# Unit 8's q and k moved to the transposing transfer, with unit 9's behind unit 7's x

## The chip, the cores and the metric

The kernel runs on one core of a Trainium2 chip. A core has five engines with their own instruction streams: TensorE (PE, matrix products into PSUM), VectorE (DVE), ScalarE (ACT), GpSimd (POOL) and SyncE (SP). They wait for one another through semaphores. Data moves between device memory and the on-chip SBUF over 16 DMA engines; in this kernel POOL issues the loads (one DMA queue, q0 in the profile) and SP issues the stores and the transposing transfers (another queue, q1). The metric is the device time of one execution in microseconds; lower is better.

## The reference

Attention inside chunks of 64 tokens, and then a feed-forward layer on its result:

```python
q_c = q.reshape(B, H, nc, chunk, D)          # B=8, H=8, S=576, D=64, chunk=64
k_c = k.reshape(B, H, nc, chunk, D)
v_c = v.reshape(B, H, nc, chunk, D)
scores = scale * np.matmul(q_c, k_c.transpose(0, 1, 2, 4, 3))
scores = scores - np.max(scores, axis=-1, keepdims=True)
attn = np.exp(scores)
attn = attn / (np.sum(attn, axis=-1, keepdims=True) + 1e-09)
out = np.matmul(attn, v_c)
...
x = out.transpose(0, 2, 1, 3).reshape(B * S, H * D)      # 4608 x 512
h = x @ w_in                                             # 4608 x 2048
g = h * (1.0 / (1.0 + np.exp(-beta * h)))
return g @ w_out                                         # 4608 x 512
```

## The kernel before

The 4,608 tokens are cut into 18 units of 256 tokens (units 0 to 17); two units make a block of 512 tokens (blocks 0 to 8). Unit u belongs to block u // 2, so units 6 and 7 make block 3, units 8 and 9 block 4.

A unit's attention goes through these steps:

- `load_qk` and `load_v`: POOL issues transfers that read q, k and v of the unit from device memory and turn them into fp16 tiles (`qu`, `ku`, `vbig`). The q and k tiles have four buffers each, so the loads of unit u + 4 wait until the tiles of unit u have been transposed; `emit_T(u)` ends with `loads_to(u + 4)`.
- `emit_T`: q and k are transposed so that the head dimension lies on partitions (`qT`, `kT`, three buffers each). There are two ways. Up to unit XU - 1 DVE does it with two stream transposes of 32x32 squares (L164), and q and k are loaded in the layout for that, two neighbouring tokens in one row (L112). From unit XU on SP issues two transposing transfers (`dma_start_transpose`, L159), and the loads use another layout, with 128 tokens on partitions (L106).
- `emit_sc`: the scores. With the squares of the first way PE needs 64 matmuls, each over 32 rows, two accumulating into one result (L232). With the second way it needs 32 matmuls over 64 rows (L219). ACT then takes the exponential (L241 or L225) into `et`.
- `emit_pv`: weights times v, with a column of the sum (L256 for units 8 and up; `xe` and `x` in PSUM). The scores and this product share one PSUM tile, tag "s".
- `emit_norm`: DVE divides by the sums and leaves `x16`.
- `emit_xt_dma`: SP issues two transposing transfers per unit (L348) that bring x into the layout `xt` that the feed-forward layer reads.

A block's feed-forward layer has 16 tiles: `emit_m(j, m)` is four matmuls of 128x512 over `xt` and w_in (L372, `hps`), the gate on ACT (L384) and DVE (L360), into `gt`. The second layer of the previous block runs at the same time: `emit_prod(j - 1, p, t)`, seven products p with two halves t each (a Strassen-like scheme that saves one product of eight), eight matmuls of 128x256 per half (L585, `ya` and `yb`; `acc` in block 1). A half takes 0.87 us on PE, a tile the same.

The order is written out by hand. For each block j from 1 on, `items` is a list of (due, rank, item), due being a fraction of the block; it is sorted by due and rank, and items with the same pair keep the order in which they were added. All engines receive their instructions in that order, each its own part. Tile m of a middle block is due at m0 + (1 - m0) * m / 16; half t of the i-th product at 0.98 * (2 * i + t) / 14. For blocks 3 to 5 the table `ATT` places the attention of units 8 to 17; unit u's entry there also places `("T", u + 3)` for u from 8 on, so units 11 and up get their transposes from there. Units 6 to 10 are placed one by one in block 2's list.

SP works off its queue in order: for block 2 that is, before the change, unit 6's x (78.38 us), unit 9's kT and qT (81.25, 82.58), unit 7's x (87.76), a store, unit 10's kT and qT (92.84, 94.54), a store, unit 11's (99.04, 102.38).

Of the kernel before, what the change touches and what calls it, by code (L numbers as in the profile page):

```python
# [15 lines left out]
def kernel(  # L16
# [59 lines left out]

    blocks = [(u, 2) for u in range(0, NU, 2)]
    NB = len(blocks)
    XU = 9
    WV = 8  # L80
    QB = 6
    unit_block = {}
# [15 lines left out]
    def load_qk(u):  # L98
        for src, dst, nm in ((q, q_t, "qu"), (k, k_t, "ku")):
            t = qk_p.tile([128, H, 2, D], FP16, tag=nm, name=nm)  # L100
            if u >= XU:
                dst[u] = t
# [49 lines left out]
    def emit_T(u, which=("kT", "qT")):  # L152
        for nm in which:
# [3 lines left out]
            dst[u] = t  # L157
            if u >= XU:
                nc.sync.dma_start_transpose(  # L159
# [50 lines left out]
    def emit_sc(u, split=False):  # L210
        qt, kt = qT.pop(u), kT.pop(u)
        sc = ps_s[0].tile([128, 2, H, CH], FP32, tag="s", name="sc")
        if u >= XU:
            qx, kx = (t.rearrange("p h s e -> p (h s e)").rearrange("p (j c t) -> p j c t", j=H, c=2)
# [29 lines left out]
    def emit_pv(u, halves=(0, 1)):  # L244
        et = et_t[u]
        if u >= WV:
# [3 lines left out]
            for n in (7, 0, 1, 2, 3, 4, 5, 6):  # L250
                for r in range(2):
# [3 lines left out]
                    for c in range(2):  # L255
                        nc.tensor.matmul(  # L256
                            out=o[64 * c:64 * c + 64],
                            lhsT=(et[64 * r:64 * r + 64, g % 2, 4 * s + 2 * c + g // 2, :] if u >= XU
                                  else et[64 * r:64 * r + 64, s, 4 * c + g, :]),
# [354 lines left out]
    with tc.manual_schedule():  # L614
# [123 lines left out]
        for j in range(1, NB):  # L738
            if j == 3:
                ps_open.pop().__exit__(None, None, None)  # L740
                ps_open.pop().__exit__(None, None, None)
                ps_open += [tc.tile_pool(name=n, bufs=1, space=bass.MemoryType.PSUM) for n in ("ps_y", "ps_t")]
                ps_y.append(ps_open[-2].__enter__())
                ps_s[0] = ps_open[-1].__enter__()
            items = []
            if j == 1:
                items += [(0.04 * m, 0, ("h", m)) for m in range(8)]
                items += [(0.32 + 0.0820 * (m - 8), 0, ("m", m)) for m in range(8, KFF)]
                items += [(0.30, 3, ("T", 4)), (0.49, 2, ("sc", 4)), (0.70, 2, ("pv", 4)), (0.71, 3, ("norm", 4, 0)),
                          (0.80, 3, ("norm", 4, 1)), (0.56, 3, ("Th", 5, "kT")), (0.61, 3, ("Th", 5, "qT"))]  # L750
                items += [(c, 3, ("wt", i)) for i, c in ((1, 0.47),)]
            else:
                m0 = {2: 0.36, 4: 0.09}.get(j, 0.02)
                if j < QB:
                    items += [(m0 + (1 - m0) * m / KFF, 0, ("m", m)) for m in range(KFF)]
                else:
                    lane = LANE[2 if j == QB else j == NB - 1]
                    cost = [1 if it[0] == "q" and it[2] == 3 else 2 for it in lane]
                    for n, it in enumerate(lane):
                        c, e, f = (0.98 * sum(cost[:n + d]) / sum(cost) for d in (0, 1, 2))  # L760
                        items.append((c, 0, it))
                        if it[0] == "m":
                            items.append((c + 0.04, 3, ("mg", it[1])))
                        elif it[0] == "last":
                            pass
                        elif it[2] == 2:
                            if it[1] == 3:
                                f = e
                            items += [(e - 0.002, 2, ("qs", it[1], 2)), (f - 0.001, 2, ("qs", it[1], 1)),
                                      (f + 0.03, 3, ("qt", it[1], 0))]  # L770
                        elif it[2] == 3:
                            items += [(c + 0.001, 2, ("qs", it[1], 0)), (c + 0.04, 3, ("qt", it[1], 1))]
                    if j == QB:
                        items.append((0.01, 6, ("open",)))
                        items += [(0.011+0.001*n, 6, ("tx", QB, n)) for n in range(4)]
                    if j + 1 < NB:
                        items += [(0.70 + 0.06 * n, 5, ("tx", j + 1, n)) for n in range(4)]
                for i, p in enumerate((1, 2, 6, 5, 7, 3, 4)):
                    for t in range(2):
                        w = 1.06 if j == NB - 1 else 0.98  # L780
                        items.append(((0.002 if j >= QB else 0) + w * (2 * i + t) / 14, 1, ("prod", p, t)))
                if j == NB - 1:
                    for i, c in ((2, 0.72), (0, 0.80), (1, 0.86)):
                        items.append((c, 4, ("pre", i)))
                for i in range(4):
                    s0 = (0.01, 0.08, 0.28, 0.36)[i] if j == 2 else 0.005 + 0.07 * i
                    if j >= QB:
                        s0 = (0.08, 0.15, 0.33, 0.48)[i] if j == QB else (0.003, 0.10, 0.33, 0.48)[i]
                    items.append((s0, 4, ("sum", i)))
                if j == 2:  # L790
                    items += [(c, 3, ("wt", i)) for i, c in ((2, 0.36), (3, 0.55))]
                    items += [(0.07, 2, ("sc", 5)), (0.08, 2, ("xp", 4, 0)), (0.12, 2, ("xp", 4, 1)),
                              (0.17, 2, ("pv", 5)), (0.18, 3, ("norm", 5, 0)), (0.19, 3, ("norm", 5, 1)),
                              (0.27, 3, ("T", 6)), (0.53, 3, ("T", 7)), (0.60, 3, ("T", 8)), (0.61, 3, ("T", 9)), (0.80, 3, ("T", 10)),
                              (0.30, 2, ("xp", 5, 0)), (0.32, 2, ("xp", 5, 1))]
                for jw, i, c, d in ((3, 2, 0.10, 0.22), (4, 1, 0.21, 0.22), (4, 3, 0.10, 0.22)):
                    if jw == j:
                        items += [(c + d * n, 5, ("ws", i, n)) for n in range(4)]
                for u, a0, w in ATT.get(j, ()):
                    items += att_items(u, a0, w)  # L800
            items.sort(key=lambda it: it[:2])
            for _, _, it in items:
                if it[0] == "m":
                    emit_m(j, it[1])
                elif it[0] == "h":
                    emit_m(j, it[1], 256, 256)
                elif it[0] == "prod":
                    emit_prod(j - 1, it[1], it[2])
                elif it[0] == "pre":
                    emit_sum(j, it[1], 0, 8 if it[1] == 2 else 4)  # L810
                elif it[0] == "sum":
                    emit_sum(j - 1, it[1])
                elif it[0] == "sc":
                    emit_sc(it[1])
                elif it[0] == "pv":
                    emit_pv(it[1], (0, 1) if len(it) == 2 else (it[2],))
                elif it[0] == "norm":
                    emit_norm(it[1], it[2])
                    if it[1] not in (4, 5):
                        emit_xt_dma(it[1], it[2])  # L820
                elif it[0] == "xp":
                    emit_xt_pe(it[1], it[2])
                elif it[0] == "wt":
                    emit_wt(it[1], (1,))
                elif it[0] == "last":
                    emit_prod(j, it[1], it[2])
                elif it[0] == "q":
                    emit_q(j, it[1], it[2])
                elif it[0] == "qs":
                    emit_q_silu(j, it[1], it[2])  # L830
                elif it[0] == "qt":
                    emit_q_scale(j, it[1], it[2])
                elif it[0] == "mg":
                    emit_mg(j, it[1])
                elif it[0] == "ws":
                    emit_ws(it[1], it[2])
                elif it[0] == "open":
                    ps_open.pop().__exit__(None, None, None)
                    ps_open.append(tc.tile_pool(name="ps_r", bufs=2, space=bass.MemoryType.PSUM))
                    ps_p[0] = ps_open[-1].__enter__()  # L840
                    while att_open:
                        att_open.pop().__exit__(None, None, None)
                    qs_p.append(ctx.enter_context(tc.tile_pool(name="qh", bufs=3)))
                    qs_p.append(ctx.enter_context(tc.tile_pool(name="qs", bufs=1)))
                    osl_p.append(ctx.enter_context(tc.tile_pool(name="osl", bufs=6)))
                elif it[0] == "tx":
                    emit_tx(it[1], it[2])
                elif it[0] == "Th":
                    emit_T(it[1], (it[2],))
                elif it[1] < NU:  # L850
                    emit_T(it[1])
# [39 lines left out]
```

## Time and profile before

| | us |
|---|---|
| median of three runs | 275.39 (275.33 to 276.52) |
| the profiled execution's own time | 276.16 |
| its span, first to last instruction | 274.4 |
| PE busy | 266.0 |
| DVE busy | 209.7 |
| ACT busy | 167.5 |
| POOL busy | 95.4 |
| granted TensorE clock | 1.000 |

The profile is one execution. Times within it are microseconds from the start of its span; the span is 1.8 us shorter than the execution's own time, and that execution is 0.8 us above the median of the runs. PE's matmuls are pipelined, so in a timeline the start of the next group, and not the end of one, tells what a group costs. "q0 software_dynamic" in the DMA view is the queue of POOL's loads, "q1 hardware_dynamic" that of SP's transfers; the columns are packets, MB, and the time that the packets took as a share of 16 engines' time (packets overlap, so shares over 100% occur).

Where the attention of the units lies on PE: scores of unit 8 at 96.26, 9 at 105.35, 10 at 115.86, 11 at 125.51, 12 at 134.28, 13 at 144.79, 14 at 155.30, 15 at 163.21, 16 at 171.99 and 17 at 179.90. First tiles: block 3 at 96.97, block 4 at 126.77, block 5 at 154.35.

### The profile page before, as it was taken

Reading aid. Unit: us, or ns where it says so; the run is one execution under the profiler, and the core shown is the slowest. Engines: PE = TensorE matmul, PEld = TensorE weight load, DVE = VectorE, ACT = ScalarE, POOL = GpSimd, SP = SyncE. Lnnn points to the kernel's source line nnn. Section 1 sums busy time; section 2 is a strip of 40 time slices with the busy share of each in tenths; the row PEclk is TensorE's granted clock in tenths of the full one; section 3 lists DMA queues with packets and bytes.
Section 4 is the critical chain, followed back from the end, with each engine's and each line's share of the span. In section 5 each row is a group of like instructions: output and inputs, shape, how many; then the busy total and the mean of one; then the engine's idle time right before and its main releaser. Section 6 shows DMA issues by size and latency. Waiting matters only on the chain.

```text
span 274.4 us, 7822 instructions
## 1 busy us (share of the span) xinstructions
PE 266.0 (97%) x3237; PEld 184.9 (67%) x3237; DVE 209.7 (76%) x394; ACT 167.5 (61%) x300; POOL 95.4 (35%) x122
## 2 busy tenths in 40 slices
PE   7789999999999999999999999999999999999995
PEld 3565445857656666666666666668887887788874
DVE  3558755899998688677977887659888778877951
ACT  3278515886555566556655656567778496759621
POOL 8954387579639955323436210000000000000000
PEclk9999999999999999999999999999999999999999
DMA  9999999999999999999999999966112102110223
GB/s 137 164 194 202 192 174 178 245 169 169 169 164 155 159 173 153 193 145 141 155 154 193 134 143 201 153 155 118 38 41 76 41 0 79 38 41 1 78 79 115
DMA packets 141763, 36.43 MB, mean 133 GB/s; under 512 B 125856, under 2 KB 141216, under 8 KB 141728
## 3 DMA queue, kind: packets, MB, share of 16 engines
q0 software_dynamic: 99136, 18.10, 83.0%
q1 hardware_dynamic: 42592, 17.84, 36.4%
q8 instruction: 25, 0.41, 0.6%
q14 instruction: 10, 0.08, 0.1%
HBM read 36.71 MB, written 9.44 MB: 168 GB/s over the span
## 4 chain that ended last, share of the span: by engine, by line
PE 67%; DMA 14%; DVE 10%; POOL 5%; issue 2%; ACT 2%; DVEq 0%; POOLq 0%
PE hps L372 23%; PE ya L585 14%; PE yb L585 14%; PE qx L484 5%; DMA wout<-in_moe_w_out_dram 5%; PE qz L484 4%; PE acc L585 4%; DMA qu<-in_q_dram 3%; DMA win<-in_moe_w_in_dram 3%; DMA ku<-in_k_dram 3%; DVE sm L436 3%; DVE gt L360 2%; POOL vbig L120 2%; PE sc L219 1%; POOL qu L112 1%
## 5 line engine op out<-in xcount | busy, mean ns | idle before, releaser
L372 PE MATMUL hps<-xt,win 128*128 128x512 f16 (+1 forms) x488 | 106.1, 355 | 0.9 <-DMA win<-in_moe_w_in_dram 0.7
L384 ACT ACTIVATE sg<-hps,bt 128x512 f32<-128x512 f32 (+1 forms) x111 | 69.5, 635 | 34.3 <-PE hps L372 31.9
L360 DVE SCALAR_TENSOR_TENSOR gt<-sg,hps 128x512 f16<-128x512 f32 (+1 forms) x111 | 67.7, 617 | 27.1 <-ACT sg L384 26.2
L372 PEld LDWEIGHTS <-win 128*128 128x128 f16 x488 | 46.2, 98 | 32.3 <-DMA win<-in_moe_w_in_dram 1.2
L585 PEld LDWEIGHTS <-sm 128*128 128x128 f16 x512 | 49.5, 98 | 12.2 <-issue 0.3
L585 PEld LDWEIGHTS <-gt 128*128 128x128 f16 x384 | 36.8, 98 | 10.6 <-DVE gt L527 0.6
L120 POOL DMA_DIRECT2D vbig<-in_v_dram x40 | 34.1, 870 | 21.8 <-DMA ku<-in_k_dram 6.3
L106 POOL DMA_DIRECT2D qu<-in_q_dram x20 | 17.1, 873 | 20.6 <-DMA qT<-qu 6.0
L513 ACT ACTIVATE hq<-hq,bs 128x256 f32<-128x256 f32 (+1 forms) x36 | 19.9, 610 | 5.5 <-DVE hq L506 5.5
L527 DVE TENSOR_SCALAR gt<-hq,rb 128x512 f16<-128x512 f32 x36 | 16.2, 481 | 6.0 <-ACT hq L513 5.3
L106 POOL DMA_DIRECT2D ku<-in_k_dram x20 | 17.1, 883 | 10.2 <-DMA qu<-in_q_dram 5.1
L436 DVE TENSOR_TENSOR sm<-gt 128x2048 f16<-128x2048 f16 (+1 forms) x17 | 19.6, 1155 | 0.3
L585 PE MATMUL yb<-wt,sm 128*128 128x256 f16 x152 | 19.7, 273 | 0.1
L585 PE MATMUL ya<-wt,sm 128*128 128x256 f16 x152 | 19.7, 273 | 0.0
L484 PEld LDWEIGHTS <-ws 128*128 128x128 f16 x144 | 14.1, 98 | 1.6
L241 ACT ACTIVATE et<-sc 128x1024 f16<-128x1024 f32 (+1 forms) x10 | 8.3, 852 | 10.5 <-PE sc L232 10.4
L397 PE MATMUL ops<-wout,gt 128*128 128x512 f16 x64 | 14.7, 380 | 0.0
L585 PE MATMUL yb<-wout,gt 128*128 128x256 f16 x104 | 13.9, 273 | 0.2
L585 PE MATMUL ya<-wout,gt 128*128 128x256 f16 x104 | 13.6, 273 | 0.0
L506 DVE TENSOR_TENSOR hq<-qz,hq 128x512 f32<-128x512 f32 x18 | 12.3, 683 | 1.1 <-ACT hq L503 0.8
L503 ACT COPY hq<-qx 128x512 f32<-128x512 f32 x18 | 10.5, 581 | 2.9 <-PE qx L484 2.7
L278 DVE TENSOR_TENSOR x<-x,rx 128x512 f16<-128x512 f32 (+1 forms) x20 | 11.9, 620 | 0.3
(100 smaller groups left out, 354.3 us busy)
## 6 DMA issues: line engine op xcount, KB each, us to landing
out_dram<-osb SPq DMA_DIRECT2D x32, 256.0 KB, 2.9
vbig<-in_v_dram POOLq DMA_DIRECT2D x32, 128.0 KB, 7.6
qu<-in_q_dram POOLq DMA_DIRECT2D x18, 128.0 KB, 11.5
ku<-in_k_dram POOLq DMA_DIRECT2D x18, 128.0 KB, 8.3
win<-in_moe_w_in_dram POOLq DMA_DIRECT2D x8, 256.0 KB, 9.5
wout<-in_moe_w_out_dram POOLq DMA_DIRECT2D x4, 512.0 KB, 12.2
qu<-in_q_dram POOLq DMA_DIRECT2D x5, 256.0 KB, 6.5
ku<-in_k_dram POOLq DMA_DIRECT2D x5, 256.0 KB, 6.8
```

The source lines that it names most:

```text
L106: nc.gpsimd.dma_start(out=tv[off:off + n, sp], in_=src[b, :, s:s + n, :].rearrange("h p d -> p h d"),)
L120: nc.gpsimd.dma_start(out=vbig[off:off + n, i % NV, :, 0:D], in_=v[b, :, s:s + n, :].rearrange("h p d -> p h d"),)
L360: nc.vector.scalar_tensor_tensor(out=gt_t[j][:, m, c0:c0 + n], in0=sg[:, 0:n], scalar=1.0, in1=hps[:, 0:n], op0=ALU.add, op1=ALU.mult,)
L372: nc.tensor.matmul(out=hps[:, 0:n], lhsT=w_in16[m // 2][:, kk, (m % 2) * 128:(m % 2) * 128 + 128], rhs=xr[:, c0 // CH:(c0 + n) // CH, 2 * ...
L384: nc.scalar.activation(out=sg[:, 0:n], in_=hps[:, 0:n], func=ACTF.Tanh, scale=bt[:, m:m + 1])
L397: nc.tensor.matmul(out=ops, lhsT=gt_t[j][:, kk, t * 128:(t + 1) * 128], rhs=w_out16[kk // 4][:, kk % 4, :], start=(kk == 0), stop=(kk == K ...
L436: nc.vector.tensor_tensor(out=sm[i][:, lo:hi, :], in0=a, in1=b, op=op)
L484: nc.tensor.matmul(out=dst[:, s, :], lhsT=lhsT, rhs=rhs, start=(p in (1, 2, 5) and s == 0 and kk == 0), stop=(s == 1 and kk == 1), skip_gr ...
L506: nc.vector.tensor_tensor(out=o, in0=x if p == 7 else z, in1=o, op=ALU.add)
L513: nc.scalar.activation(out=o, in_=src, func=ACTF.Silu, scale=bs[:, m:m + 1])
L527: nc.vector.tensor_scalar(out=gt_t[j][:, m, :], in0=hq[:, b].rearrange("p c q -> p (c q)"), scalar1=rb[:, m:m + 1], scalar2=None, op0=ALU. ...
L585: nc.tensor.matmul(out=dst, lhsT=lhsT, rhs=rhs, start=(p in (1, 2, 5) and kk == 0 and (t == 0 or last)), stop=(kk == 7 and (t == 1 or last ...
```

## The change

Three edits:

1. XU goes from 9 to 8: unit 8's q and k are loaded in the other layout and transposed by two transposing transfers on SP; its scores are 32 matmuls.
2. In block 2's list, `("T", 8)` is due at 0.53, right behind `("T", 7)`, and `("T", 9)` at 0.79, behind unit 7's last `norm` and its x.
3. Block 3's tiles begin at m0 = 0.09, where they began at 0.02.

```diff
-    XU = 9
+    XU = 8
...
-                m0 = {2: 0.36, 4: 0.09}.get(j, 0.02)
+                m0 = {2: 0.36, 3: 0.09, 4: 0.09}.get(j, 0.02)
...
-                              (0.27, 3, ("T", 6)), (0.53, 3, ("T", 7)), (0.60, 3, ("T", 8)), (0.61, 3, ("T", 9)), (0.80, 3, ("T", 10)),
+                              (0.27, 3, ("T", 6)), (0.53, 3, ("T", 7)), (0.53, 3, ("T", 8)), (0.79, 3, ("T", 9)), (0.80, 3, ("T", 10)),
```

In the instruction streams this gives: on PE 32 score matmuls in place of 64, and at the start of block 3 the order product half, scores of unit 8, product half, first tile, weighted sum of unit 8 (before: product half, scores, first tile, product half, second tile, weighted sum); on DVE two stream transposes fewer; on POOL four load instructions for unit 8's q and k in place of two; on SP the order unit 6's x, unit 8's kT and qT, unit 7's x, a store, unit 9's, unit 10's, a store, unit 11's, and from there as before.

## The prediction

> **What bounds the kernel now.** I read the page first: the busy times, then the row of DMA slices.
>
> ```profile
> PE 266.0 (97%) x3237; PEld 184.9 (67%) x3237; DVE 209.7 (76%) x394; ACT 167.5 (61%) x300; POOL 95.4 (35%) x122
> ...
> DMA  9999999999999999999999999966112102110223
> ```
>
> PE is idle for 8.4 us of the span of 274.4, so the end is set by the sum of PE's work plus whatever makes PE wait. The DMA engines are busy in the first 26 of 40 slices (to 178 us), which is the whole stretch that the change touches. So there are two resources without room. Next, the view by stretches of time, to see where PE idles:
>
> ```profile
> 80.00:90.00 10.00, 9.88 (x150) 5.87 (x149) 8.96 (x16) 5.18 (x8) 7.74 (x11) 1.00 1.91 156
> 90.00:100.00 10.00, 10.00 (x154) 6.24 (x151) 7.10 (x11) 6.53 (x10) 9.53 (x11) 1.00 2.16 170
> ```
>
> Second column PE: 9.88 and 10.00 of 10 us, at a granted clock of 1.00. There is no idle time left to win here, only PE work to remove. PE's timeline shows what the scores of a unit cost in each form (unit 8 by L232, unit 9 by L219):
>
> ```profile
> 95.30 1.04 PE L585 MATMUL yb<-wout,gt 128*128 128x256 f16 x8
> 96.26 0.71 PE L232 MATMUL sc<-qT,kT 32*64 32x64 f16 x64
> 96.97 1.02 PE L372 MATMUL hps<-xt,win 128*128 128x512 f16 x4
> ...
> 104.39 1.04 PE L585 MATMUL yb<-wt,sm 128*128 128x256 f16 x8
> 105.35 0.44 PE L219 MATMUL sc<-qT,kT 64*64 64x64 f16 x32
> 105.73 1.04 PE L372 MATMUL hps<-xt,win 128*128 128x512 f16 x4
> ```
>
> Starts count, as ends overlap. Then SP's timeline, the one queue that issues all transposing transfers (first column start, second how long SP was held):
>
> ```profile
> 81.25 1.23 SPq L159 DMA_TRANSPOSE kT<-ku  x1
> 82.58 1.77 SPq L159 DMA_TRANSPOSE qT<-qu  x1
> 87.76 4.28 SPq L348 DMA_TRANSPOSE xt<-x  x2
> 92.09 0.58 SPq L539 DMA_DIRECT2D out_dram<-osb  x1
> 92.84 1.60 SPq L159 DMA_TRANSPOSE kT<-ku  x1
> 94.54 3.69 SPq L159 DMA_TRANSPOSE qT<-qu  x1
> ...
> 167.75 2.70 SPq L159 DMA_TRANSPOSE kT<-ku  x1
> 170.56 2.60 SPq L159 DMA_TRANSPOSE qT<-qu  x1
> ```
>
> These are units 9, 10 and 17, with unit 7's x between. From 92.84 to about 154 SP runs with hardly a gap. Last, the DMA view for single stretches: 84 to 85 us, 106 to 110, 160 to 162 (packets, MB, share):
>
> ```profile
> q1 hardware_dynamic: 1029, 0.25, 120.5%
> ...
> q0 software_dynamic: 1716, 0.22, 82.5%
> q1 hardware_dynamic: 1646, 0.41, 78.9%
> ...
> q0 software_dynamic: 2405, 0.30, 238.0%
> ```
>
> The transposes' queue (q1) alone moves some 1,000 packets per us, the loads' queue (q0) alone 1,200; with work in both, each gets about 412 to 430. They take turns, so each slows the other.
>
> **The change part by part.** *PE.* 64 score matmuls of unit 8 (L232) become 32 (L219). From the product's start to the next group: 96.97 - 95.30 = 1.67 with L232, 105.73 - 104.39 = 1.34 with L219. Saved: 0.33 us, all on the path, since PE is full.
>
> *DVE* loses the two stream transposes of unit 8 (0.70 + 0.67 at 83.66). PE did not wait for DVE after them, so 0; the bound on the other side is a rival below.
>
> *POOL.* Unit 8's loads are four issues instead of two: units 8 and 9 took 1.81 and 3.63 us, so 1.8 us more. POOL waits 1.52 us before unit 10's loads (72.64) and 4.36 before unit 11's (82.26); that hides it. In packets, 2,048 of 256 B become 4,096 of 128 B: at 961 in 1.5 us (61 to 62.5) and 2,446 in 2 us (71 to 73) that is 3.2 against 3.35 us; from 82 to 84 the loads' queue moves nothing, which hides the 0.15. Without that cover it would delay later loads by 0.15 us.
>
> *SP.* Two transposes are added in all. Unit 8's take the place of unit 9's at 81.25, with the same neighbours, and land as those did (kT after 4.3 us; the queue was empty again by 87), against unit 8's scores at 96.26: 0. Unit 9's move behind unit 7's x, to 92.84, and units 10 and 11 and everything later on SP slide back. In unit 10's present place qT takes 10.4 us to land, at 104.9; unit 9's scores are due at 105.35 - 0.33 = 105.0. But POOL now holds unit 13's loads (94.15) until unit 9's q has been read, so fewer loads compete and I expect it near 102.5: 0, at worst 0.3.
>
> *The slide.* One unit's q and k are 2,048 packets (84 to 87 us shows 2,085 for unit 9). They are put into a stretch where both queues are full up to 169 us. Price of the slide, both ends: alone, 2,048 / 1,029 = 2.0 us; taking turns throughout, 2,048 / 412 = 5.0 us on the transposes' queue, and on the loads' 5.0 - 2,048 / 1,200 = 3.3. The rows from 105 to 170 look like the dear end, while POOL's hold makes unit 9's second half run alone; and unit 17's k, whose landing releases the issue at 167.75, now loses the stretch 160 to 162 in which it had the engines to itself. I take 4.2, between 3.3 and 5.0.
>
> *What has room for it.* Landings are issue plus the view's time to landing; dues are PE's starts less 0.33 saved and 0.3 to get going. Block 4's first tile: x of unit 9 lands at 113.1 + 8.5 = 121.6, due 126.1, room 4.5. Block 5's: 142.5 + 7.4 = 149.9, due 153.7, room 3.8. Scores of unit 15: 157.9, due 162.6, room 4.7. Unit 16: 158.62 + 10.3 = 168.9, due 171.4, room 2.5. Unit 17: 170.56 + 6.5 = 177.1, due 179.3 (its L219 group started at 179.90), room 2.2. Stalls do not add: once PE has waited, the later dues move with it. So the stall is the largest lack: 4.2 - 2.2 = 2.0 us at unit 17's scores (ends: 0 with a slide of 2.0, 2.8 with 5.0). After that PE's work is the same as before and the end moves by all of it.
>
> *Block 3's tiles.* The first tile now starts at 95.30 + 0.87 + 0.47 + 0.87 = 97.5, where unit 7's x has landed (90.8 + 5.4 = 96.2). The price is a shorter cover for unit 8's exponential: one product and one tile between scores and weighted sum. Unit 11 has that order already (125.51 to 127.73) with no gap on PE: 0, at worst 0.3.
>
> *Sum:* -0.33 + 2.0 = +1.7 us. In the profiled execution the span would go from 274.4 to 276.1; its own time is 276.16, with 1.8 around the span, so 277.9. The median of the runs shown, 275.39, lies 0.77 below that execution; put on the median, the forecast is 277.1 us.
>
> [...]
>
> **The rivals.** *The slide is hidden.* If the extra packets run mostly while the loads are held (unit 13's, for some 4 us after 100), the slide is 2.0, under the smallest room, 2.2. Then only the saved PE time shows: 275.39 - 0.33 = 275.06. For it: SP waits for other things than room at 157.28 and 167.75 and could catch up. Against: those two waits are for k to land, and the loads slide too.
>
> *The slide breaks in at several places* (slower still): if each loss feeds back, because late transposes hold POOL's next loads (the buffers have four units), the slide grows to some 6 or 7 us. It decides from 4.5 on, where blocks 4 and 5 start late as well; 6.5 - 2.2 - 0.33 = +4.0: 279.4. For it: the loads of units 13 to 16 land 11 to 19 us after issue, already. Against: unit 14's loads were issued at 105.5, 27 us ahead of their transposes.
>
> *DVE was pacing PE.* If the 1.37 us taken off DVE came back on PE, -0.33 - 1.37 = 273.7. Against: PE 9.88 and 10.00 of 10 in these stretches.
>
> That the change does not do what it says I rule out: the changed program's instruction order has 32 matmuls for unit 8 and the two more transposes.
>
> **How the numbers follow.** Forecast (277.1, own range 276.3 to 278.3) 0.50; hidden (275.06) 0.32; several places 0.14; DVE 0.04. A measurement of this kernel tells from no change about 0.5%, 1.4 us. Of the forecast's 0.50, 0.08 lies under 276.8. Slower: 0.42 + 0.14 = 0.56; same: 0.32 + 0.08 = 0.40; faster 0.04. The range reaches from just under the hidden case to near the several-places case: 274.9 to 279.0.
>
> **What would show it.** Right: unit 8's scores in about 0.47 us of PE; unit 9's transposes issued near 92.8 and its scores unhindered; unit 17's issued near 171 to 173 instead of 167.75, and a PE gap of 1 to 3 us ahead of its scores, the only large one. Wrong: no gap there (hidden); gaps at the first tiles of blocks 4 and 5 (several places); or a gap at unit 9's scores, which would mean that its place behind unit 7's x is too late.

## The result, and the profile after

| | before | after |
|---|---|---|
| median of six runs, us | 275.64 (275.33 to 276.52) | 278.04 (277.12 to 281.62) |
| profiled execution's own time, us | 276.16 | 278.86 |
| its span, us | 274.4 | 277.1 |

After over before is 1.0081, with a 95% interval of 1.0054 to 1.0109: slower by 0.5 to 1.1%. Ratios, here and below, leave out executions in a slower state, of which 281.62 is one. The medians differ by 2.4 us, where 1.7 were forecast; the median of after lies in the forecast's range and 0.9 above the forecast. Where the time went is another matter.

The page of after, the same two rows as before:

```profile
PE 266.9 (96%) x3205; PEld 185.0 (67%) x3205; DVE 208.9 (75%) x392; ACT 167.3 (60%) x300; POOL 97.2 (35%) x124
...
DMA  9999999999999999999999999965112102110223
```

32 matmuls fewer, and the row of nines is the same. The view by stretches of after (columns: stretch, its length, then busy time and number of instructions of PE, PEld, DVE, ACT and POOL, the granted clock, DMA share, GB/s):

```profile
80.00:90.00 10.00, 9.88 (x150) 5.82 (x148) 7.98 (x15) 5.65 (x8) 6.73 (x9) 1.00 1.92 150
90.00:100.00 10.00, 10.00 (x127) 6.53 (x126) 7.65 (x15) 6.08 (x11) 5.26 (x6) 1.00 2.22 167
120.00:130.00 10.00, 8.54 (x120) 5.74 (x119) 6.96 (x13) 5.29 (x9) 2.92 (x4) 1.00 1.73 142
150.00:160.00 10.00, 8.37 (x104) 5.16 (x105) 7.16 (x13) 5.27 (x11) 3.90 (x5) 1.00 1.60 164
```

Before's lines of the last two stretches:

```profile
120.00:130.00 10.00, 10.00 (x157) 6.64 (x146) 8.49 (x19) 5.51 (x11) 2.93 (x4) 1.00 1.77 138
150.00:160.00 10.00, 10.00 (x127) 6.58 (x126) 8.59 (x18) 6.44 (x13) 3.40 (x4) 1.00 1.76 142
```

PE lost 1.46 and 1.63 us in two stretches where it was full before; from 80 to 120, from 130 to 150 and from 160 to 190 it is as full as it was. PE's timeline of after names the spots: unit 8's scores, then the first tiles of blocks 4 and 5 (in square brackets the idle time just before, and what the profile puts it down to):

```profile
94.50 1.04 PE L585 MATMUL yb<-wout,gt 128*128 128x256 f16 x8
95.47 0.45 PE L219 MATMUL sc<-qT,kT 64*64 64x64 f16 x32
95.85 1.05 PE L585 MATMUL yb<-wout,gt 128*128 128x256 f16 x8
...
127.28 1.02 PE L372 MATMUL hps<-xt,win 128*128 128x512 f16 x4 [1.46 <-DMA xt<-x]
...
156.65 1.02 PE L372 MATMUL hps<-xt,win 128*128 128x512 f16 x4 [1.63 <-issue]
```

From product to next group, unit 8's scores take 95.85 - 94.50 = 1.35 us, where the forecast had 1.34. The two waits are for x: of unit 9 (block 4) and of unit 11 (block 5). For the second the profile names nothing ("issue"), but the landing below does. SP's timeline of after:

```profile
80.45 2.18 SPq L159 DMA_TRANSPOSE kT<-ku  x1
82.74 2.51 SPq L159 DMA_TRANSPOSE qT<-qu  x1
86.96 4.27 SPq L348 DMA_TRANSPOSE xt<-x  x2
...
92.03 1.49 SPq L159 DMA_TRANSPOSE kT<-ku  x1
93.62 3.16 SPq L159 DMA_TRANSPOSE qT<-qu  x1
...
114.66 4.37 SPq L348 DMA_TRANSPOSE xt<-x  x2
...
146.25 2.59 SPq L348 DMA_TRANSPOSE xt<-x  x2
...
171.09 2.82 SPq L159 DMA_TRANSPOSE kT<-ku  x1
```

Units 8 and 9 are where they were expected. Of unit 11's x, the second transfer by itself, from the view of the tile `xt` (start of the issue, then time to landing); after first:

```profile
L348 SPq DMA_TRANSPOSE xt<-x x1: 1229/1229/1229, 147.6 to 147.6; - x1
...
DMA to landing us min/median/max: 8.9/8.9/8.9
```

and before:

```profile
L348 SPq DMA_TRANSPOSE xt<-x x1: 1249/1249/1249, 142.5 to 142.5; - x1
...
DMA to landing us min/median/max: 7.4/7.4/7.4
```

Unit 11's x lands at 147.6 + 8.9 = 156.5 instead of 149.9, and PE's tile starts 0.15 us later. In the same way unit 9's second transfer (117.3 + 9.9, before 113.1 + 8.5) lands at 127.2 instead of 121.6.

**One table for all runs.** It has one execution of each kernel, the profiled one. Executions differ by 1 us and more in when PE gets to its first unit, so landings are best counted from PE's scores of unit 5, the same work in every kernel (65.73 us before, 64.94 after). The first two rows tell when PE reaches the first tile of blocks 3, 4 and 5 if it waits for nothing: before, 96.97, 126.77 and 154.35, less 65.73; in the changed order block 3's comes one product half later (96.73 - 64.94 in after) and the others 0.33 earlier. "To unit 17" is from unit 5's scores to unit 17's, which leaves out what happens at the start and the end. The runs e1 to e12 are told below; the two rows of needs don't hold for blocks 4 and 5 in e6 and block 3 in e8, which begin later by design. A pair is a unit's two transposing transfers, kT and qT.

| | unit 7's x | unit 9's x | unit 11's x | to unit 17 | PE waits |
|---|---|---|---|---|---|
| needed, before | 31.2 | 61.0 | 88.6 | | |
| needed, after | 31.8 | 60.7 | 88.3 | | |
| before | 30.5 | 55.9 | 84.2 | 114.17 | none |
| after | 29.7 | 62.3 | 91.6 | 117.25 | 1.46, 1.63 |
| e1, unit 9's pair early | 33.5 | 57.3 | 87.6 | 115.67 | 1.67 (block 3) |
| e2, before with unit 9's pair late | 30.4 | 58.8 | 88.3 | 114.15 | none |
| e3, before with one more pair | 31.7 | 63.5 | 92.5 | 118.32 | 0.47, 1.94 (blocks 3, 4) |
| e4, e1 with unit 11's x first | 34.1 | 57.5 | 80.8 | 118.02 | 2.34 (block 3) |
| e5, unit 8 only | 31.1 | 56.7 | 85.2 | 114.11 | none |
| e6, after with later tiles | 30.1 | 61.9 | 92.2 | 120.26 | 1.39, 2.84 (scores of units 12, 15) |
| e7, after with unit 11's x first | 30.6 | 60.1 | 84.3 | 117.34 | 1.51, 0.50, 1.27 (scores of units 9, 14, 16) |
| e8, before with block 3's first tile later | 31.4 | 58.6 | 87.9 | 114.11 | none |
| e9, after without stores | 30.6 | 54.1 | 80.9 | 113.85 | none |
| e10, before without stores | 31.7 | 53.8 | 80.8 | 114.72 | 0.55 (block 3) |
| e11, before with half a pair | 30.6 | not shown | 89.2 | 114.81 | 0.51 (block 5) |
| e12, one more pair at 170 us | 30.3 | 56.1 | 83.9 | 114.15 | none |

Take landing less need, row by row: after, 62.3 - 60.7 = 1.6, and then 91.6 - 88.3 - 1.6 = 1.7, because the first wait had moved the second need; e1 33.5 - 31.8 = 1.7; e4 34.1 - 31.8 = 2.3; e3 31.7 - 31.2 = 0.5 and 63.5 - 61.0 - 0.5 = 2.0. These are the measured waits within 0.15 us, landings being rounded. Where x lands before the need, there is none.

The table also tells how far one execution can be trusted. In e5, e8 and e12 SP's queue has as many pairs ahead of unit 11's x as before, and at the same places. Yet unit 9's x lands 0.2 to 2.7 us later than before, and unit 11's between 0.3 earlier and 3.7 later; the far end is e8, where PE came to unit 5 2.2 us later than before. So differences of landings under 4 us, between single executions, show nothing by themselves.

After's books: to unit 17 it took 117.25 - 114.17 = 3.08 us more, which is -0.33 for the matmuls and 3.41 for two waits of 1.46 and 1.63. From product to tile PE took 127.28 - 124.78 = 2.50 and 156.65 - 153.98 = 2.67 us there; in e9, without the waits, 0.88 and 0.87. So the two places cost 1.62 and 1.80, 0.16 and 0.17 more than the idle times that the profile shows. PE came to unit 5 0.79 us earlier in that execution, and 0.4 more came behind the start of the last matmuls: 3.08 - 0.79 + 0.4 = 2.7, the difference of the spans.

### The profile page after: what moved, and what is told of

Read it like the earlier page. It is cut to its first block, busy times and chain, and to the rows that moved or that the text cites. A ratio compares the mean times of both kernels' runs of the same rounds, so it can differ in the third digit from the quotient of the medians.

```text
span 277.1 us, 7764 instructions
## 1 busy us (share of the span) xinstructions
PE 266.9 (96%) x3205; PEld 185.0 (67%) x3205; DVE 208.9 (75%) x392; ACT 167.3 (60%) x300; POOL 97.2 (35%) x124
## 3 DMA queue, kind: packets, MB, share of 16 engines
q1 hardware_dynamic: 44704, 18.37, 36.9%
## 4 chain that ended last, share of the span: by engine, by line
PE 72%; DVE 11%; DMA 9%; POOL 3%; issue 2%; ACT 2%; DVEq 0%; POOLq 0%
PE hps L372 27%; PE yb L585 13%; PE ya L585 13%; PE qx L484 5%; PE qz L484 4%; DMA xt<-x 4%; PE acc L585 4%; PE ops L397 3%; DMA qu<-in_q_dram 3%; DVE sm L436 3%; DMA win<-in_moe_w_in_dram 3%; DVE gt L360 2%; DVE x L313 1%; PE sc L219 1%; POOL vbig L120 1%
## 5 line engine op out<-in xcount | busy, mean ns | idle before, releaser
L106 POOL DMA_DIRECT2D qu<-in_q_dram x22 | 18.7, 862 | 20.1 <-DMA qT<-qu 9.7
L106 POOL DMA_DIRECT2D ku<-in_k_dram x22 | 18.8, 872 | 7.6 <-DMA ku<-in_k_dram 3.9
L241 ACT ACTIVATE et<-sc 128x1024 f16<-128x1024 f32 (+1 forms) x9 | 7.3, 833 | 9.5 <-PE sc L232 9.4
```

What stands on the lines that cost most here:

```text
L106: nc.gpsimd.dma_start(out=tv[off:off + n, sp], in_=src[b, :, s:s + n, :].rearrange("h p d -> p h d"),)
```

## The experiments

Ratios are against runs of the kernel before on the same chip: median 275.90 for e1 to e4, 275.54 for e5 to e8, 275.65 for e9 to e12.

**e1, unit 9's pair ahead of unit 7's x.** The changed kernel with one number put back:

```diff
-(0.53, 3, ("T", 8)), (0.79, 3, ("T", 9)),
+(0.53, 3, ("T", 8)), (0.61, 3, ("T", 9)),
```

> The changed kernel with unit 9's q and k transposed right behind unit 8's (due 0.61 in block 2, ahead of unit 7's x) and all else kept. Theory A (the place: 2,048 packets were moved from a stretch in which the transposes' queue ran empty, 83 to 90 us, into one in which it is full until 174): the first tiles of blocks 4 and 5 wait under 0.5 us each instead of 1.46 and 1.63, time 275.0 to 275.8. Rival B (one more pair of transfers costs the same wherever it stands): both waits stay at 1 to 2 us, 277.5 to 278.2. Rival C (unit 7's x now comes late behind two pairs): a wait at block 3's first tile of 1 to 2 us takes their place, 276 to 277.

Median 278.04 (276.86 to 280.66), ratio 1.0090 [1.0058, 1.0122]. PE's timeline has one wait after 60 us:

```profile
98.85 1.02 PE L372 MATMUL hps<-xt,win 128*128 128x512 f16 x4 [1.67 <-issue]
```

It is block 3's first tile: unit 7's x is now issued behind two pairs (88.93, before 87.76) and lands at 98.7. Blocks 4 and 5 don't wait. This is theory C's wait with a median in B's range. An early place makes unit 7's x late, which the change's place for unit 9's pair avoids; the cost comes out elsewhere and is as large.

**e2, the late place without the extra pair.** The kernel before with unit 9's pair behind unit 7's x, unit 8 left on DVE:

```diff
-(0.60, 3, ("T", 8)), (0.61, 3, ("T", 9)),
+(0.60, 3, ("T", 8)), (0.79, 3, ("T", 9)),
```

> The kernel before with the one edit that unit 9's q and k are transposed behind unit 7's x (due 0.79); unit 8 stays on VectorE, so the number of transfers is that of before. Theory A (the place): unit 9's packets again lie in the full stretch, waits at the first tiles of blocks 4 and 5 as in the changed kernel, 278.0 to 278.6 (the 0.33 us of PE are not saved). Rival B (one more pair): no more pairs than before, 275.3 to 275.9.

Median 276.29 (275.33 to 280.34), ratio 1.0013 [0.9994, 1.0031]: no difference, and no wait, as rival B had it. Unit 9's x lands 2.9 us later than before and unit 11's 4.1 (table), 0.3 us ahead of the need. That looks like the price of the place; but e8, which moves nothing in SP's queue, has 2.7 and 3.7 in its execution. Whether the late place by itself delays the x stays open.

**e3, one more pair.** The kernel before, with unit 10's k and q transposed a second time into tiles that are filled with other values later (the extra result is not used):

```diff
+for i in range(2 if u == 10 else 0):
+    nc.sync.dma_start_transpose(
+        out=ws[1][2 * (nm == "qT") + i].rearrange("p a b -> p (a b)").rearrange("p (j t) -> p j t", t=128),
+        in_=a.rearrange("p h r d -> p (h r d)")[:, 512 * i:512 * i + 512],
+    )
```

> The kernel before with a second, unused copy of unit 10's transposed q and k (four transfers of 512 packets on SP, 2,048 packets in all, into tiles that are overwritten later); nothing else is touched. Theory A: 2,048 more packets in the full stretch, so x of units 9 and 11 lands 5 to 7 us later and the first tiles of blocks 4 and 5 wait some 1 to 2 us each: 277.5 to 279. A rival by which the loss comes from the order of PE, from unit 8's form or from block 3's due times leaves this kernel at 275.3 to 276.0.

Median 280.11 (279.10 to 280.54), ratio 1.0146 [1.0118, 1.0174]. As many packets (2,048; after's page has 44,704 on q1, before's 42,592), without any part of the change, cost 4.2 us, more than theory A had; the waits are at blocks 3 and 4, where it expected blocks 4 and 5. PE's timeline, where L377 is the tile's line:

```profile
129.30 1.25 PE L377 MATMUL hps<-xt,win 128*128 128x512 f16 x4 [1.94 <-DMA xt<-x]
...
132.74 2.22 PE L377 MATMUL hps<-xt,win 128*128 128x512 f16 x8
```

Unit 9's x comes 7.6 us later than before. Behind the wait, eight matmuls take 2.22 us, where they take 1.89 at a granted clock of 1.00 (after, 129.49 us); from 132 to 136 us the granted clock was 0.83 (last section). SP's timeline shows the four extra issues (L164 here), which hold SP for 8.8 us:

```profile
92.77 1.90 SPq L159 DMA_TRANSPOSE kT<-ku  x1
94.72 4.53 SPq L164 DMA_TRANSPOSE ws<-ku  x2
99.36 2.67 SPq L159 DMA_TRANSPOSE qT<-qu  x1
102.07 4.26 SPq L164 DMA_TRANSPOSE ws<-qu  x2
```

The extra pair reads unit 10's tiles, so POOL's loads of unit 14, which go into the same buffers, wait for it as well: they are issued at 112.80 us, before at 105.50.

**e4, e1 with unit 14's pair behind unit 11's x:**

```diff
-it.append((a0 + (0.45 * w if u == 9 else 0.005), 3, ("T", u + 3)))
+it.append((a0 + (0.45 * w if u in (9, 11) else 0.005), 3, ("T", u + 3)))
```

> As the first run, and unit 14's q and k are issued behind unit 11's x instead of ahead of it. Theory A with SP's order as the second half of it (unit 11's x lies finished on DVE by 134 us and waits on SP for unit 14's pair): the first tile of block 5 does not wait at all, 275.0 to 275.4, and unit 14's scores still come in time. Rival: unit 14's pair is now the late one and its scores wait 1 us or more, 276 to 277.

Median 278.29 (277.35 to 280.40), ratio 1.0068 [1.0042, 1.0094]. Unit 11's x lands 6.8 us earlier than in e1, so the exchange does that. But block 5 did not wait in e1 either, and the median lies above both expectations. Block 3's wait remains, and PE's timeline puts it down to the wrong thing:

```profile
100.05 1.02 PE L372 MATMUL hps<-xt,win 128*128 128x512 f16 x4 [2.34 <-DVE sm L436]
...
103.06 2.76 PE L372 MATMUL hps<-xt,win 128*128 128x512 f16 x8
```

Unit 7's x landed at 99.9, 0.15 us before the tile: it was x, as in e1.

**e5, unit 8 on the transposing transfer, unit 9 back on DVE.** The changed kernel with `u >= XU` replaced in four places:

```diff
+def by_dma(u):
+    return u >= XU and u != 9
```

> The changed kernel, with unit 8 on the transposing transfer as there but unit 9 back on DVE's stream transposes (64 score matmuls): as many pairs of transposing transfers as before, only another unit's. PE's work is that of before (unit 8 saves 0.33 us, unit 9 gives it back). Theory 'the count of pairs': the transfers after unit 7's x stand where they stood before (second issue of unit 9's x near 114 to 115, unit 17's pair near 167 to 169), no wait at the first tiles of blocks 4 and 5, time 275.3 to 276.2. Rival 'the layout or the place of unit 8's pair': the waits at blocks 4 and 5 stay and the time is 277.5 to 278.5.

Median 275.24 (275.03 to 276.17), ratio 0.9992 [0.9979, 1.0005], no wait, landings within 1.0 us of before. As many pairs as before, no cost: neither unit 8's other loads nor its pair's place do harm.

**e6, later tiles.** The changed kernel with the first tiles of blocks 4 and 5 two product halves later:

```diff
-m0 = {2: 0.36, 3: 0.09, 4: 0.09}.get(j, 0.02)
+m0 = {2: 0.36, 3: 0.09, 4: 0.23, 5: 0.16}.get(j, 0.02)
```

> The changed kernel, with the first tiles of blocks 4 and 5 two product halves (about 1.7 us) later: m0 0.23 for block 4 (was 0.09) and 0.16 for block 5 (was 0.02). Theory 'late x of units 9 and 11': the transfers land when they did, but the tiles come 1.7 us later, so the waits of 1.46 and 1.63 us vanish and the time is the one of before less the 0.33 us saved, 275.0 to 275.8. Rival 'the transfers' lack of room shows wherever it can': the waits move on, to the scores of unit 16 or 17 or the next first tile, and the time stays above 277.

Median 277.71 (276.97 to 281.60), ratio 1.0088 [1.0056, 1.0120]. The tiles wait no more; the profiled execution, the longest of its five runs, waits at the scores of units 12 and 15 instead:

```profile
132.86 0.45 PE L219 MATMUL sc<-qT,kT 64*64 64x64 f16 x32 [1.39 <-DMA qT<-qu]
...
164.94 0.65 PE L219 MATMUL sc<-qT,kT 64*64 64x64 f16 x32 [2.84 <-DMA qT<-qu]
```

In that execution the waits move on, as the rival had it, though to other units; the other executions have no trace, but their times show that nothing was won. The first tiles and the scores behind them are fed by one queue that is behind.

**e7, the changed kernel with unit 11's x ahead of unit 14's pair** (the edit of e4, unit 9's pair late):

> The changed kernel, with unit 14's pair of transposes behind unit 11's x in SP's queue instead of ahead of it. Theory: unit 11's x lands 4 to 6 us earlier, block 5's wait (1.63 us) vanishes, block 4's (1.46 us) stays as nothing ahead of it moved, unit 14's scores are not late: 276.0 to 277.0. Rival: POOL's loads, which wait for unit 14's q and k to be read, come later, and the wait turns up at the scores of units 15 to 17: 277.5 or more.

Median 276.15 (275.39 to 278.66), ratio 1.0048 [1.0018, 1.0079]. The median is where the theory had it. The only trace is of the longest execution, and it shows other waits than the theory's: there unit 9's x comes in time too (60.1 after unit 5's scores), and PE waits for q of units 9, 14 and 16:

```profile
104.67 0.45 PE L219 MATMUL sc<-qT,kT 64*64 64x64 f16 x32 [1.51 <-DMA qT<-qu]
...
156.05 0.45 PE L219 MATMUL sc<-qT,kT 64*64 64x64 f16 x32 [0.50 <-DMA qT<-qu]
...
174.08 0.45 PE L219 MATMUL sc<-qT,kT 64*64 64x64 f16 x32 [1.27 <-DMA qT<-qu]
```

The one at unit 16 is the rival's; the one at unit 9 nobody had. Nothing ahead of unit 9's pair differs from the changed kernel, so which consumer comes up short also varies from one execution to the next; the spread of 3.3 us over nine runs says the same.

**e8, block 3's first tile alone.** The kernel before with `3: 0.09` added to `m0`.

> The kernel before, with block 3's first tile behind two product halves (m0 0.09 in place of 0.02) and nothing else. Both theories: no wait added, none removed, the same PE work: 275.3 to 276.2. If unit 8's exponential loses its cover, a wait of 0.3 us or more shows before unit 8's weighted sum and the time is above 276.2.

Median 275.43 (275.12 to 278.32), ratio 1.0009 [0.9986, 1.0031]. This edit costs nothing. The profiled execution is the longest; it lost its time ahead of unit 5's scores (67.95 us, before 65.73; last section), and PE doesn't wait behind unit 5's scores.

**e9 and e10, without stores.** The 16 stores of blocks 1 to 4 are left out, of the changed kernel (e9) and of the kernel before (e10):

```diff
-while late:
-    emit_store(*late.pop(0))
+while late:
+    key = late.pop(0)
+    if key[0] in (1, 2, 3, 4):
+        oq_t.pop(key)
+        continue
+    emit_store(*key)
```

> The changed kernel without the 16 stores (256 KB each) of blocks 1 to 4: their rows of the output are never written. Everything else is as in the changed kernel. Theory 'the DMA engines have no room for one more pair between 62 and 178 us': with 4 MB taken out of that stretch the transposes land earlier, no wait at the first tiles of blocks 4 and 5, and what is left is the PE saving: 0.33 us under the kernel before, 274.9 to 275.4. Rival 'the order in SP's queue, or POOL's loads held behind unit 9's q, makes the x late': order and hold are the same here, so waits of 1 us and more stay and the time is over 276.5.

> The kernel before without the same 16 stores: the control for the run above. No wait to remove after 60 us, so no change: 275.2 to 275.8 in both theories. If it were more than 0.5 us faster, the stores cost something else than room, and the run above must be read against this one.

e9: median 275.73 (275.19 to 276.15), ratio 0.9998 [0.9984, 1.0011]; e10: 275.91 (275.40 to 279.85), 1.0005 [0.9986, 1.0023]. e10's trace is of its longest execution, which came to unit 5's scores 3.1 us later than before (68.87 us) and has a wait of 0.55 at block 3. Of e9, the two stretches in which the changed kernel lost its time:

```profile
120.00:130.00 10.00, 10.00 (x128) 6.53 (x126) 8.44 (x18) 6.30 (x12) 3.27 (x5) 1.00 1.83 130
150.00:160.00 10.00, 10.00 (x126) 6.32 (x124) 8.04 (x15) 6.63 (x13) 0.00 (x0) 1.00 1.72 144
```

With SP's order of pairs as in the changed kernel, and POOL's hold too (unit 13's loads issued at 102.26 us, in after at 103.19), the waits are gone. What is left is the saving: 113.85 - 114.17 = -0.32 us to unit 17. The whole execution shows 0.18 of it against e10, which is within the spread; 275.73 is 0.3 above what was expected. With the stores gone, the x of units 9 and 11 land at 54.1 and 80.9 with the change and at 53.8 and 80.8 without it (table), and SP issues unit 11's x 71.4 us behind unit 5's scores in e9 (136.68 - 65.25) and 71.1 in e10 (139.97 - 68.87): the added pair no longer delays them.

The stores take two things at once, though. They use the DMA engines (from 62 to 178 us q1 moved 10.21 MB in after and 8.00 in e9), and each holds SP for 0.53 to 0.70 us: in after 2.3 us from the four ahead of unit 9's x, behind unit 7's, and 4.0 from the seven ahead of unit 11's. The landings came 8.2 and 10.7 us earlier in e9, so SP's time is not all of it; but it alone could have covered waits of 1.6 and 3.3 us. No run parts the two.

**e11, half a pair.** As e3, but unit 10's k alone (1,024 packets).

> The kernel before with half of the unused extra pair: unit 10's k alone is transposed a second time (1,024 packets in place of 2,048). Theory 'rooms': half a pair slides the later transposes by about 2.5 to 3.3 us, under the room of 3.8 and 4.5 us at blocks 5 and 4: no wait, 275.3 to 276.3. Rival 'no room at all, each packet costs': half of what the whole pair cost (4.5 us), 277.3 to 278.0.

Median 277.45 (276.71 to 277.60), ratio 1.0060 [1.0040, 1.0079]: the rival's number. In the profiled execution, the shortest of four, PE waits once, 0.51 us at block 5; unit 11's x lands at 146.1 + 8.4 = 154.5, 0.6 past the need. So there was room, 4.4 us, but half a pair slid that x by 5.0 us, not by 2.5 to 3.3. To unit 17 it took 0.64 us more than before (180.08 - 65.27); the rest of the median's 1.8 us is not in this profile.

**e12, a whole pair at the end.** The kernel before, with unit 17's k and q transposed a second time, each right behind the first, from 169.66 us on.

> The kernel before with a whole unused extra pair, but behind unit 17's pair, near 174 us, where the loads have ended (last load packet at 169.7 us): unit 17's q and k are transposed a second time, into free tiles. Theory 'full stretch': here the DMA engines have room, and the only transfers behind it are the x of units 16 and 17, needed 60 us later: no wait, 275.3 to 276.2. Rival 'an extra pair costs wherever it is' (through SP's issue time or what it does to other engines): 277.5 or more, as the same pair did at unit 10.

Median 275.96 (275.60 to 276.80), ratio 1.0012 [0.9998, 1.0025]. The pair that cost 4.2 us at unit 10 costs nothing here that can be measured. Two things differ from e3: the loads are over (POOL's busy time in e12 is 0.00 from 160 us on, and in before the loads' queue moved one packet from 169.7 to 185 us), and no transfer with an early need stands behind the pair. SP's timeline suggests that the first matters too (L165 is the extra pair):

```profile
166.59 2.98 SPq L159 DMA_TRANSPOSE kT<-ku  x1
169.66 3.06 SPq L165 DMA_TRANSPOSE kT<-ku  x1
172.83 1.25 SPq L159 DMA_TRANSPOSE qT<-qu  x1
174.13 1.33 SPq L165 DMA_TRANSPOSE qT<-qu  x1
```

The extra pair, in two issues of 1,024 packets, holds SP for 3.06 and 1.33 us, 4.4 in all. In e3, in four issues of 512 packets, it was 8.8.

**Together.** One more pair costs time in the stretch that the loads fill, with transfers behind it that are needed soon (e3, with no other part of the change); with as many pairs as before there is no cost (e5), nor at the end (e12); taking the stores out of that stretch cures it (e9), be it through the DMA engines or through SP's time; moving the consumers or the order shifts the wait (e1, e4, e6, e7). No version was faster than before: e5 is level with it. Holding the stores back until 180 us instead of leaving them out was not tried; it would need more output tiles than the six there are.

## Why the prediction was right or wrong

- *What bounds the kernel, and PE's saving.* Right: 1.35 us for 1.34, and -0.32 in e9 for -0.33.
- *DVE, POOL's issues, unit 8's pair, block 3's tiles at nothing.* Right: e5 and e8 show no difference. The rival of a DVE that paces PE is out: e9 has the same two stream transposes fewer and won 0.32 us, not 1.7.
- *Unit 9's own scores unhindered, at worst 0.3.* Right in the profiled execution of after, but e7's execution has 1.51 there, in the same place of the queue. The worst case was too small.
- *The slide, 4.2 between 3.3 and 5.0.* This is the step that failed: one slide for all consumers, priced by the packets that are added. At unit 9's x it was 6.4 and at unit 11's 7.4, both above the dear end. e3, which adds the pair and moves nothing, has 7.6 and 8.3 (the longest of its four executions), so 5.0 looks too little even for a pair that is added without a move. A price per packet can't be read from the traces: 1,024 packets go with 5.0 us at unit 11's x in e11, 2,048 with 3.4 in e1 and 8.3 in e3, each in one execution and with what PE's own waits added. At unit 17's pair the issue is 4.1 us later, 171.09 - 64.94 against 167.75 - 65.73, as forecast; but by then PE itself had waited 3.4, so that agreement proves nothing. The prediction also put the move of unit 9's pair at nothing for those behind it; e2's 2.9 and 4.1 could be its price, but e8 has nearly the same without the move.
- *The rooms, 4.5 and 3.8.* Right: with 0.3 to get going (the forecast's own allowance; in after block 5's tile starts 0.15 us behind the landing) and 0.33 saved, the table's 61.0 - 55.9 and 88.6 - 84.2 give the same.
- *"Stalls do not add", the stall is the largest lack.* Right, once each consumer has its own slide: unit 11's x came 91.6 - 88.3 = 3.3 us after the need, unit 9's 1.6, and PE lost 3.4 in all at the two. Behind these two waits unit 17's scores had 3.4 us more, and there was no third.
- *The sum.* Forecast 2.0 us of waiting at unit 17's scores; measured 3.4 in two places, none of it there. What happened is the rival "breaks in at several places", with its mark, gaps at blocks 4 and 5, but at 278.0 and not 279.4, because it was priced as a lack of 6.5 - 2.2 at unit 17, and not by the rooms of 4.5 and 3.8 at the two places that it named. That the number of the forecast was near is luck: two errors met, a slide that was too small, and a room of 2.2 us at a consumer that then never waited.

An extra pair has no one price here: in e12 it costs no time that can be measured (ratio 1.0012); in e3, beside the loads, unit 9's x lands 7.6 us later with the same pair.

Open: why the slide was more than the packets' price. SP's time for its issues is one candidate. Another is POOL, which holds later loads until an added or moved pair has been read: unit 13's in after (103.19 us, before 94.15), unit 14's in e3. Such a hold is not enough for a wait, as e2 (104.85) and e9 (102.26) have it too, and no wait; whether it adds to the slide, no run tells.

## What to carry to other kernels

When a transfer is added to or moved within a queue that stays busy, list every consumer behind it with its landing and its need, each with its own slide: the smallest room is not always where the wait comes out (here it was 2.2 us, at unit 17's scores, and PE waited where the rooms were 4.5 and 3.8), and a move within the queue decides who waits (block 3 for 1.67 us in e1, blocks 4 and 5 for 1.46 and 1.63 in after). Compare landings over more than one execution before a difference of a few us is put down to an edit. Where waits only change their place under local repairs, ask for the amount of work in the stretch, and test it by taking other work out of it.

## What the runs showed of the hardware

**Behind waits of 1.94 to 2.84 us the granted clock fell, and 1.7 us more were lost.** In the full stretch behind unit 5's scores, waits of 1.39 (e6), 1.46 and 1.63 (after), 1.51 (e7) and 1.67 us (e1) left the granted clock at 1.00. After 1.94 (e3), 2.34 (e4) and 2.84 us (e6) it fell. The view by stretches, the clock being the third number from the end; e3:

```profile
128.00:132.00 4.00, 2.70 (x41) 1.53 (x42) 1.79 (x3) 0.69 (x1) 0.94 (x2) 0.75 1.77 157
132.00:136.00 4.00, 4.00 (x23) 2.37 (x22) 3.58 (x10) 1.89 (x4) 2.48 (x4) 0.83 1.76 134
```

e4:

```profile
100.00:104.00 4.00, 3.95 (x47) 2.23 (x48) 2.13 (x7) 1.21 (x3) 1.33 (x2) 0.68 1.56 175
104.00:108.00 4.00, 4.00 (x25) 2.35 (x24) 3.51 (x6) 1.71 (x3) 1.92 (x3) 0.90 1.71 187
```

e6:

```profile
164.00:168.00 4.00, 3.06 (x40) 1.74 (x41) 0.10 (x1) 1.52 (x2) 0.00 (x0) 0.62 1.81 155
168.00:172.00 4.00, 4.00 (x56) 2.47 (x54) 2.23 (x6) 2.00 (x6) 0.00 (x0) 0.96 1.63 158
```

The lost clock is the same each time: 4 us times (0.25 + 0.17), (0.32 + 0.10) and (0.38 + 0.04), 1.68 us. It closes e3's books: 0.47 + 1.94 + 1.68 is 4.1 of the 4.15 us more to unit 17. The length of a wait does not tell it alone. In the first 20 us, where PE is busy for 2.70 to 3.54 of each 4 us in before and the granted clock stays at 1.00, e2 lost the same 1.68 us (clock 0.68 and 0.90 from 8 to 16 us), though PE was as busy as before just ahead of it: 2.75 of 4 us from 4 to 8, before 2.70. In e8 the mean granted clock was 0.987, which over 276.6 us is 3.6 us; from 80 to 190 us it was 1.00, the longest wait that the profile lists for PE is 1.2 us, and PE came to unit 5 2.2 us later than before. What sets the clock is not shown.

**The row of nines is not a measure of room.** From 62 to 178 us, the DMA view of after:

```profile
DMA  9999999999999999999999999999999999999999
...
DMA packets 98173, 18.78 MB, mean 162 GB/s; under 512 B 95342, under 2 KB 98158, under 8 KB 98158
```

and of e9:

```profile
DMA  9999999999999999999999999999999999994502
...
DMA packets 97778, 16.51 MB, mean 142 GB/s; under 512 B 97763, under 2 KB 97763, under 8 KB 97763
```

With 2.27 MB less, 36 of 40 slices are still full, and yet unit 11's x lands 10.7 us earlier (91.6 and 80.9 in the table). So the row of nines alone does not tell that another transfer would come late; landings against needs do.
